# A new issue list for the same operations: fewer zero matmuls, fewer changes of tile shape on TensorE

## The chip, the core and the metric

The kernel runs on one core of one Trainium2 chip. The time is device time in microseconds (us), and a kernel's time is the median of its runs. A core has these engines, each with a queue of its own that it works through in order: TensorE (in the profile PE, its weight loads PEld), VectorE (DVE), ScalarE (ACT), GpSimd (POOL) and SyncE (SP). In this kernel SP issues every DMA. An engine waits at an instruction until the semaphores of that instruction are met, and everything behind it in the same queue waits too.

## The reference

Two unrelated layers whose outputs stand side by side in the last axis, all in float32, with 2048 positions and 576 channels each:

```
# A: a state-space convolution, N = 128 modes per channel
dt = exp(log_dt); A = -exp(log_A_real) + 1j*A_imag; C = (C_real + 1j*C_imag) * dt
K = 2*Re( sum_n C[d,n] * exp(A[d,n]*dt[d]*pos) )           # 2048 taps for each channel
y = irfft( rfft(u, 4096) * rfft(K, 4096) )[:2048] + u * D_skip

# B: linear attention, 32 heads of 18
q, k, v = x @ wqkv
phi(z) = concat( softmax(z @ w_phi), softmax(-(z @ w_phi)) )
o = phi(q) @ (phi(k)^T v)  /  ( phi(q) @ sum(phi(k)) + 1e-6 )
out = concat( y, o @ wo )
```

## The kernel before

`body` does not issue anything while it builds. It registers 2459 operations in a `Plan`, each with its engine (some with a second engine that may do it instead), what it reads and writes, and, for TensorE, the shape of the array tile that its matmuls use (`mode`, rows by columns: 128x128, 64x128, 128x32, 64x32, 32x64, 32x128, 128x64). The text `ORDER` at L992 then says in which order they are issued. `Plan.run` walks through it, and each engine gets its own operations in the order of that list. One word of `ORDER` reads like `1521@60:7`: the number is the operation, an `x` behind it gives it to its second engine, the digits behind `@` are the PSUM banks (0 to 7) for the PSUM tiles that it is the first to use, and the number behind `:` is a count of zero matmuls that `emit` puts on TensorE directly ahead of it:

```
for word in ORDER.split():
    word, _, fill = word.partition(":")
    word, _, at = word.partition("@")
    k = int(word.rstrip("x"))
    ...
    self.emit(k, o, o[12][0] if word[-1] == "x" else o[0], int(fill or 0), at)
# in emit, with fill > 0:
    for _ in range(fill):
        self.matmul(t[0:cols, 0:n], self.zero.t[0:rows, 0:cols], self.data.t[0:rows].bitcast(BF16)[:, 0:n], ...)
```

A zero matmul (L237 in the profile) multiplies a tile of zeros with the identity matrix, 256 columns, in the tile shape of the operation behind it and into that operation's own PSUM bank. It changes no result, it needs that bank to be free, and it needs none of the operation's inputs. All other matmuls stand at L295 (`mm`), transpositions at L549 and L577.

The operations, in units that the list interleaves freely:

- *fold* (four of them, at the start and in the middle): the weights of keys, values, queries and output are split in a high and a low part (`wh`, `wl` and `vh`, `vl`), the first and third multiplied with `w_phi` on the way (25 matmuls, `fT` with the staged weights).
- *key* and *query*, 16 tiles of 128 positions each. A tile loads x, splits it into `x9`, and runs two halves of 14 matmuls of 288 columns for each weight (the 28 of them are called a GEMM here; `gemm`, L410). A key tile then takes the double softmax (mostly DVE L434, L314, L437, L442, ACT L440, POOL L310 on `e`) and adds 32 small matmuls into the sums (k4, `e` with `v`). A query tile takes the softmax, transposes (q3, L549), multiplies with the sums (q4), divides, transposes (q5, L577) and runs the GEMM with `wo` (q6).
- *u* (16): the first half of the Fourier transform of u (`u_first`, 4 matmuls `ub` with `w1`, two copies, a DMA to DRAM).
- *par* and *group* (18 pairs of groups): powers and phases of the modes. Of a pair, g0 makes exponents on TensorE (`sel` with `mg`, three times two matmuls, 64x128), ACT takes their exp in PSUM (L811), POOL and ACT make sines (L757, L774 to L785), DVE multiplies them (L815, L816, L818, L820), and g4 (128x32) sums over the modes.
- *kfirst* (16) and *product* (16): the same transform of K, and for each of 16 sets of frequencies the load of its factors `ff` and of u and K (`ub`), transforms p1 and p2 (64x32), the product (DVE L314, `ac`), and p4 back (32x64). The `ff` tiles have two buffers.
- *last* (16): the result is read back from DRAM, l1 (64x32), a copy into `ot`, four DMAs of 73 KB each to the output (L979).

PSUM has 8 banks. A bank is reused when the copies out of it are done, so an operation on TensorE waits for its inputs and for the readers of the banks that the list gives it.

Of the kernel before, what the change touches and what calls it, by code (L numbers as in the profile page):

```python
# [992 lines left out]
0 1 2 3 1097 1093 4 68 1094 5 1096 1154 1104 1105 1107 1092 1108 1109 51 34 1095 6 27 7@0:49 20 1106 1110 1111 1112 1113 1114 1115 8 35@2 1199 1137 11  # L993
28@4 29 52 12 1116 1120 9 53x 30 36 10 54 13 22@6 32 37 21 1117 39 992 1118 1119 40 15@0 14 1074 23 31 33 1121 38 1063 1003 344 18 25 16 345 24
1004@42:11 19 26 17 41 1073 287 1127 1077 56@6 47 42 288 1078 48 1122 1124 346x 1123 57 347x 1125 43 1126 44 45 60 1396 1076 1084 1006 1128 1129 289x
1130 1080 61 49 1075 348@0 1400 46 1131 349 1079 290 1138 291@6 1132 1161 1133 1134 352 62 1081 292 295 353 296 1082 354 1085 351@2 1083 350 355x 1397
1048 294@0 59@6 1086 1399 1135 55 1136 63 268 269 1155 361 1005 64 58 356 69 71 270x 297 360 1162 1156 1157 1398 271x 65 1158 171 1087 1064@24 1066 72
1200 1163 293 273@6 272 357 66 67 73x 1159 1164 1160 1065 1088 298x 1089 50@4 299 358 1090 1168 74 1165 70 304 359 1166 1167 77@2 300 276 1139 1401
301 277 1402 362 172 173x 1169 1170 1192 302 76 274@0 1140 275 80 278 1141 1403 1091 1148 1147 279 1149 1150 174 303 1193 1201 1151@56 1172 111 1098
1171 81 82 1152@72 305 285x 1099 79@0 1180 1174 112 1173 1175 78 1177 1176 1153@35 89 1178@6 1067 1068 1194 1183 284 1202 1203 1181 1184 83 1204 1195  # L1000
# [94 lines left out]
```

## Time and profile before

| | |
|---|---|
| median of 3 runs | 545.37 us (543.55 to 545.37) |
| the profiled execution | 545.11 us, its span 543.3 us |
| TensorE busy | 521.5 us, 96% |
| VectorE busy | 455.9 us, 84% |
| ScalarE, GpSimd busy | 382.1 us (70%), 328.8 us (61%) |
| mean granted clock of TensorE | 0.998 |
| moved by DMA | 107.01 MB |

The span runs from the first to the last instruction of one execution. Busy time is the union of an engine's instructions; a matmul's row lasts longer than the distance to the next one (the array overlaps them), so the time that an operation costs on TensorE is read from the starts of two neighbours and not from its busy time. In a row of the order of time stand the start, the length, and in brackets the idle time ahead of the row and what ended it.

### The profile page before, as it was taken

Reading aid. Unit: us, or ns where it says so; the run is one execution under the profiler, and the core shown is the slowest. Engines: PE = TensorE matmul, PEld = TensorE weight load, DVE = VectorE, ACT = ScalarE, POOL = GpSimd, SP = SyncE. Lnnn points to the kernel's source line nnn. Section 1 sums busy time; section 2 is a strip of 40 time slices with the busy share of each in tenths; the row PEclk is TensorE's granted clock in tenths of the full one; section 3 lists DMA queues with packets and bytes.
Section 4 is the critical chain, followed back from the end, with each engine's and each line's share of the span. In section 5 each row is a group of like instructions: output and inputs, shape, how many; then the busy total and the mean of one; then the engine's idle time right before and its main releaser. Section 6 shows DMA issues by size and latency. Waiting matters only on the chain.

```text
span 543.3 us, 19242 instructions
## 1 busy us (share of the span) xinstructions
PE 521.5 (96%) x8192; PEld 435.9 (80%) x8192; DVE 455.9 (84%) x716; ACT 382.1 (70%) x555; POOL 328.8 (61%) x456
## 2 busy tenths in 40 slices
PE   8999999999999989999999999999899999999995
PEld 7999899888888767888878666766689877776984
DVE  7999899898868889999989996999974889787641
ACT  4868798798559799889689977989733444343332
POOL 1173885958777775982758998997433617434300
PEclk9999999999999999999999999999999999999999
DMA  8936711244245678246664588756458789998785
GB/s 235 326 105 195 281 45 31 101 139 134 89 139 190 207 241 294 83 128 196 229 205 118 153 265 250 241 180 194 131 173 271 234 281 293 287 281 260 265 252 157
DMA packets 86163, 107.01 MB, mean 197 GB/s; under 512 B 5698, under 2 KB 70338, under 8 KB 86078
## 3 DMA queue, kind: packets, MB, share of 16 engines
q1 hardware_dynamic: 86078, 105.79, 61.5%
q8 instruction: 64, 1.05, 0.8%
q14 instruction: 21, 0.17, 0.1%
HBM read 61.22 MB, written 44.54 MB: 195 GB/s over the span
## 4 chain that ended last, share of the span: by engine, by line
PE 69%; DVE 13%; DMA 7%; ACT 4%; issue 3%; SPq 2%; POOL 1%; DVEq 0%; ACTq 0%; POOLq 0%
PE psum L295 63%; PE psum L549 3%; DMA ff<-in_ff_dram 2%; DMA dram<-zi 2%; PE psum L237 2%; DVE ac L314 1%; DVE cs L816 1%; SPq L979 1%; PE psum L577 1%; DMA cs<-dram 1%; DVE e L310 1%; DMA ub<-dram 1%; DVE e L314 1%; DVE small L434 1%; DVE small L437 1%
## 5 line engine op out<-in xcount | busy, mean ns | idle before, releaser
L295 PE MATMUL psum<-vh,x 128*128 128x288 f32 x576 | 123.6, 301 | 0.5 <-ACT ks L300 0.5
L295 PE MATMUL psum<-wh,x 128*128 128x288 f32 x576 | 124.1, 302 | 0.0
L757 POOL TENSOR_TENSOR cs<-cs,pi 128x32 int32<-128x32 int32 (+4 forms) x180 | 108.5, 608 | 8.0
L295 PEld LDWEIGHTS psum<-wh,x 128*128 128x128 f32 x576 | 94.1, 188 | 7.7 <-issue 4.2
L295 PEld LDWEIGHTS psum<-vh,x 128*128 128x128 f32 x576 | 94.0, 188 | 5.4 <-issue 3.2
L295 PE MATMUL psum<-vl,x 128*128 128x288 f32 x320 | 93.8, 295 | 0.0
L295 PE MATMUL psum<-wl,x 128*128 128x288 f32 x320 | 93.7, 295 | 0.0
L811 ACT ACTIVATE psum<-psum 128x512 f32<-128x512 f32 x108 | 59.9, 588 | 15.4 <-PE psum L295 14.9
L295 PEld LDWEIGHTS psum<-vl,x 128*128 128x128 f32 x320 | 60.2, 188 | 0.0
L295 PEld LDWEIGHTS psum<-wl,x 128*128 128x128 f32 x320 | 60.2, 188 | 0.0
L310 POOL TENSOR_TENSOR x<-zo,x 64x128 fp32r<-64x128 f32 (+1 forms) x30 | 25.4, 848 | 46.3 <-ACT x L394 35.1
L310 POOL TENSOR_TENSOR e<-e,small 128x1152 f32<-128x1152 f32 (+1 forms) x24 | 41.2, 1720 | 14.5 <-DVE small L450 7.8
L815 DVE TENSOR_TENSOR cs<-psum,cs 128x1024 f32<-128x1024 f32 x36 | 43.6, 1212 | 3.7 <-ACT psum L811 3.6
L310 POOL TENSOR_TENSOR e<-small,e 128x576 f32<-128x576 f32 x26 | 30.6, 1177 | 25.4 <-DVE small L437 23.6
L816 DVE TENSOR_TENSOR cs<-psum,cs 128x1024 f32<-128x1024 f32 x36 | 43.6, 1214 | 1.4 <-PE psum L295 1.3
L295 PE MATMUL psum<-ub,ff 64*32 64x288 f32 x1024 | 40.0, 410 | 4.3 <-DMA ff<-in_ff_dram 1.9
L295 PEld LDWEIGHTS psum<-kvb,fT 126*128 126x128 f32 (+1 forms) x320 | 38.3, 188 | 7.2 <-issue 2.9
L295 PEld LDWEIGHTS psum<-cs 128*32 128x32 f32 x2304 | 34.1, 110 | 11.2 <-issue 2.9
L295 PE MATMUL psum<-cs 128*32 128x64 f32 x2304 | 40.0, 220 | 2.6 <-DVE cs L816 0.9
L295 PE MATMUL psum<-kvb,fT 126*128 126x133 f32 (+1 forms) x320 | 41.6, 280 | 0.1
L440 ACT ACTIVATE e<-e 128x1152 f32<-128x1152 f32 x32 | 37.0, 1164 | 2.7 <-POOL e L310 1.3
L781 ACT ACTIVATE cs<-cs 128x1040 f32<-128x1040 int32 x36 | 38.3, 1064 | 0.6 <-POOL cs L776 0.4
(156 smaller groups left out, 1115.2 us busy)
## 6 DMA issues: line engine op xcount, KB each, us to landing
dram<-zi SPq DMA_DIRECT2D x32, 576.0 KB
ub<-dram SPq DMA_DIRECT2D x64, 288.0 KB
dram<-zo SPq DMA_DIRECT2D x32, 288.0 KB
zo<-in_xT_dram SPq DMA_DIRECT2D x24, 320.0 KB
zi<-dram SPq DMA_DIRECT2D x12, 576.0 KB
ub<-in_u_dram SPq DMA_DIRECT2D x16, 288.0 KB
xd<-x SPq DMA_DIRECT2D x8, 576.0 KB
x<-xd SPq DMA_DIRECT2D x8, 576.0 KB
```

The costliest lines, as they stand in the source:

```text
L237: self.matmul(t[0:cols, 0:n], self.zero.t[0:rows, 0:cols], self.data.t[0:rows].bitcast(BF16)[:, 0:n], start=not o[13], stop=not o[13], ski ...
L295: pe.matmul(o, l, r, start=start, stop=stop, skip_group_check=skip)
L310: op(eng, [c_dve(n[0]) if e == "dve" else c_pool(n[1]) for e in eng], lambda e: (dve if e == "dve" else pool).tensor_tensor(dst(), a(), b( ...
L314: op(eng, c_dve(n) if eng == "dve" else c_pool(n), lambda: e.tensor_tensor(dst(), a(), b(), op=alu), r=r, w=w, with_=with_, lock=eng == "p ...
L434: op("dve", c_dve(D), lambda: dve.tensor_reduce(two(top.t), v(), axis=AX.X, op=ALU.max, negate=True), r=[p], w=[top])
L440: op("act", c_act(1152) + 40, lambda: act.activation(e.t, e.t, AF.Exp), r=[e], w=[e], table="exp")
L549: pe.transpose(tp.t[0:m, j - j0, :], e.t[:, sign, 7 * g:7 * g + GRP[g], :].rearrange("p h f -> p (h f)"), ident.t)
L757: op("pool", c_pool(2 * n * W), lambda n=n, j=j: pool.tensor_tensor(x()[:, :, :, n:2 * n], x()[:, :, :, 0:n], pi.t[:, j:j + 2, gs].bitcast ...
L781: act.activation(cs.t[:, 1], cs.t[:, 1].bitcast(I32), AF.Sin, scale=TURN)
L811: op("act", c_act(512), lambda b=b: act.activation(b.t, b.t, AF.Exp), r=[b], w=[b], table="exp")
L815: op("dve", c_dve(64 * W), lambda: dve.tensor_tensor(F(), both(M.t), F(), op=ALU.mult), r=[M, cs], w=[cs])
L816: op("dve", c_dve(64 * W), lambda: dve.tensor_tensor(E.t[:, :, :, 32:64], both(up.t), cs.t[:, :, :, 0:32], op=ALU.mult), r=[up, cs], w=[E])
```

## The change

Only the text `ORDER` changes, all 83 of its lines. The 2459 operations, the tiles and the buffers are the same. Counted over the two lists:

| | before | now |
|---|---|---|
| zero matmuls | 118 (49 ahead of the first fold, 69 at 12 other places, up to 11 at one) | 75 (the same 49, 26 at 17 other places, 1 to 3 at one) |
| changes of tile shape from one TensorE operation to the next | 240 | 229 |
| instructions on DVE, ACT, POOL by choice of the second engine | 716, 519, 452 | 725, 511, 451 |

The first words of the list:

```diff
-0 1 2 3 1097 1093 4 68 1094 5 1096 1154 1104 1105 1107 1092 1108 1109 51 34 1095 6 27 7@0:49 20 1106 1110 1111 1112 1113 1114 1115 8 35@2 1199 1137 11
+0 1 2 1104 4 6 1073 27 1105 1093 20 1094 1107 5 1106 68 1108 34 7@6:49 1110 51 1109 8 28@0 1111 13 1112 11 1113 9 1095 1114 12 1115 29 35@2 32 1003
...
```

Most of TensorE's operations keep their place to within a few neighbours. Three places of TensorE's queue show the kinds of move.

The start, from the end of the first fold to the first key GEMM (`w1` with `ub` is u, `wh` and `wl` with `x9` the GEMM). Before:

```order
L295 MATMUL psum_73<-fT_99,cs_177 128x126 x5
L295 MATMUL psum_73<-fT_99,e_214 128x126 x5
L237 LDWEIGHTS zero_86
L237 MATMUL psum_73<-ident_84,zero_86 128x256
...
L295 MATMUL psum_73<-ub_244,w1_225 128x288 x4
L295 MATMUL psum_73<-wh_195,x9_202 128x288
L295 MATMUL psum_73<-wl_204,x9_202 128x288
```

Now, in the same queue:

```order
L295 MATMUL psum_73<-fT_106,cs_101 128x126 x4
L295 MATMUL psum_73<-fT_106,e_179 128x126 x5
L295 MATMUL psum_73<-ub_197,w1_199 128x288 x4
L295 MATMUL psum_73<-wh_182,x9_202 128x288
L295 MATMUL psum_73<-wl_188,x9_202 128x288
```

The 11 zero matmuls between fold and u are gone (the rows left out of the first list repeat its pair). On DVE, one operation of 1536 elements (`sel`, L310) that stood behind the first fold's `fT` is now done by POOL.

The middle, around the exponents of the pair of groups 8 (`sel` with `mg` is g0, `cs` with `cs` is g4, `ub` with `w1` is u, `wh` and `wl` with `x9` the query GEMMs). Before:

```order
L295 MATMUL psum_73<-ub_3031,w1_225 128x288 x4
L295 MATMUL psum_73<-sel_109,mg_1819 128x512 x4
L237 LDWEIGHTS zero_86
L237 MATMUL psum_73<-ident_84,zero_86 128x256
...
L295 MATMUL psum_73<-ub_3170,w1_225 128x288 x4
L237 LDWEIGHTS zero_86
L237 MATMUL psum_73<-ident_84,zero_86 128x256
...
L295 MATMUL psum_73<-sel_109,mg_1819 128x512 x2
L295 MATMUL psum_73<-cs_3326,cs_2976 32x64 x32
L295 MATMUL psum_73<-wh_2835,x9_3304 128x288
```

Now:

```order
L295 MATMUL psum_73<-sel_210,mg_1824 128x512 x2
L295 MATMUL psum_73<-ub_2862,w1_199 128x288 x4
L237 LDWEIGHTS zero_86
L237 MATMUL psum_73<-ident_84,zero_86 128x256
L295 MATMUL psum_73<-sel_210,mg_1824 128x512 x2
L295 MATMUL psum_73<-ub_2810,w1_199 128x288 x4
L295 MATMUL psum_73<-wh_2931,x9_3233 128x288
...
L295 MATMUL psum_73<-wl_2984,x9_3233 128x288
L295 MATMUL psum_73<-sel_210,mg_1824 128x512 x2
L295 MATMUL psum_73<-cs_3304,cs_2808 32x64 x32
```

The 8 and 7 zero matmuls there become 1 (and 2 ahead of the first `sel`), and half a GEMM (14 matmuls) of query tile 3 now stands between the second u and the last `sel`, ahead of g4.

Later, the transposition of query tile 6 (L549) between the exponents of the pair of groups 17. Before:

```order
L295 MATMUL psum_73<-ac_5307,ff_5146 64x288 x16
L295 MATMUL psum_73<-sel_109,mg_4641 128x512 x2
L549 MATMUL psum_73<-ident_84,e_4532 126x128 x4
L295 MATMUL psum_73<-sel_109,mg_4641 128x512 x2
L549 MATMUL psum_73<-ident_84,e_4532 126x128 x4
L549 MATMUL psum_73<-ident_84,e_4532 72x128 x2
```

Now:

```order
L295 MATMUL psum_73<-ac_5257,ff_5040 64x288 x16
L295 MATMUL psum_73<-sel_210,mg_4690 128x512 x4
L549 MATMUL psum_73<-ident_84,e_4501 126x128 x4
L549 MATMUL psum_73<-ident_84,e_4501 72x128 x2
L549 MATMUL psum_73<-ident_84,e_4501 126x128 x4
```

The two pairs of `sel` now stand together ahead of the three transpositions, which makes two changes of tile shape fewer there.

More of the change, by code (lines that the diff above doesn't have):

```diff
@@ L997 @@
[L997 to L1000, printed above, removed]
@@ L1073 @@
[L1073 to L1075 removed]
+0 1 2 1104 4 6 1073 27 1105 1093 20 1094 1107 5 1106 68 1108 34 7@6:49 1110 51 1109 8 28@0 1111 13 1112 11 1113 9 1095 1114 12 1115 29 35@2 32 1003
+992 30 52 1120 22@4 36 1116 1096 10 1092x 344 53 37 21 44 3 39 14@6 15 1161 47 31 23 25 33 38 40 1004@02 1097 1117 16 1154 24 26 1006 54 1076 345 1118
@@ new lines @@
+308 1049@62 1254@5 1418 1050 100 1283x 1229@67 101 1307 1051 1420 1098 225 1282 340x 226x 198@2 1421 1257 102 1258 1008 1306 1260 196@0 1261 199 103x
+1255x 197 229 1284 208 1262 1263@5 209 1265@67 1422 200 1440 1052 201 1069@20 343 1285 1314 1308 249 1264 202 1071 1313 1267@51 1439 195 1309 1070
+1423 1288 1266@06 1315 1286 104 1424 1296 203 1310 1311 309x 1316 1287 1317 1289 105 1294 98@2 1318 99 204 1312 1290 1291 250 1319 1067 109 1297
+1292@7 1300 1425 1320 1293x 1299 1426 106 1427 1103 230 310@2 1039@60 311 1484 205 1321 206 1428 108 379x 1295 1041x 1322 207x 314 107 231 313@0 232
@@ new lines @@
+402 458 389@4 1468 1010 1445@23 1527 1472 404 1528 406 1474 1535 1469 1475 405 1473 408 1012 407 1470@6 1361 1537 388 1536x 1471x 390 1478 395@0 392
+1362 1363 396 410@6 409 1476 399 1364 1365 397 1037 1477 1366 1479@2 400 1369 393 391 371@3 411 415 1368 367@4 398 374x 413 1370 459@0 414 1371 373x
+993 1367 1429 1538 412 460 368x 1372 365 1480x 1430 1373 1374 1431 372x 1376 424 1375x 461 426@6 462 370 526 416 994@02 369x 425 1432 375 417
+1519@54:2 463 1433 996x 995x 427 1044@20 1377 464 428 377 1539 1520@76:1 1045x 376 997 1434 429 1046 1548 430 1542 1541 1540 1551 1435 378 1545
@@ new lines @@
+2155 1741 1751 2046 2111 2157 1742 2162@0 1612@45 567 1724 1632 2161 604 557 558 1743 662 2163 568 517@23 1725 1633 605 2047 1635 630@0 518 1753 519
+2048 520 1744 1752x 1636 1613@46 1614@72 521 1634 1641 1637 2164 1638 629 1639@3 569 523@4 1643 1642 1644 522 2165 631 2053 1784 1646 632 2051@0 1783
+1754 1647 1640x 1735@63 457 1645 1785 1786 1648@2 606 633 1755 1787 607@7 1788 1789 524 1791x 1649 2052x 1756 570 2166@04 608 1758 1776 571 1736@72
+611@6 2167 2049@4 1777 1759 2168 1757 1761 1778 1779 1780 1781 2109 1760 609@3 1764 2050 2116 1773@01 610 1737@45 1782 1794 2110 612x 1765 1766
@@ L1076 @@
+2425@4 954 2406 2407 989@2 2426x 2428 2408 2427 2430 988 990 2429 991
 """
```

146 lines of the change are left out of this document (68 added, 78 removed).

## The prediction

> **What bounds the kernel now.** I read the page's busy times and its chain first, then the busy time by stretches, then TensorE's rows in order of time at the places that the list changes.
>
> ```profile
> PE 521.5 (96%) x8192; PEld 435.9 (80%) x8192; DVE 455.9 (84%) x716; ACT 382.1 (70%) x555; POOL 328.8 (61%) x456
> PEclk9999999999999999999999999999999999999999
> PE 69%; DVE 13%; DMA 7%; ACT 4%; issue 3%; SPq 2%; POOL 1%; DVEq 0%; ACTq 0%; POOLq 0%
> ```
>
> TensorE is busy 96% of the span and makes 69% of the chain. DVE's 13% of the chain says that TensorE often stands behind DVE. By stretches (columns: length, then busy us and instructions of PE, PEld, DVE, ACT, POOL; clock, DMA share, GB/s):
>
> ```profile
> 8.90:100.00 91.10, 90.40 (x1281) 84.77 (x1282) 86.44 (x131) 72.80 (x99) 53.32 (x86) 1.00 0.49 162
> 200.00:250.00 50.00, 47.89 (x626) 41.44 (x616) 47.06 (x92) 44.98 (x62) 37.59 (x53) 1.00 0.59 191
> 250.00:300.00 50.00, 48.60 (x761) 40.71 (x766) 47.41 (x83) 42.75 (x63) 30.97 (x52) 1.00 0.54 170
> 300.00:350.00 50.00, 48.78 (x927) 34.19 (x912) 44.46 (x63) 41.99 (x65) 45.84 (x60) 1.00 0.79 239
> 350.00:400.00 50.00, 47.05 (x983) 33.67 (x985) 48.11 (x69) 42.41 (x64) 36.35 (x47) 1.00 0.48 151
> ```
>
> Up to 100 us TensorE has almost no idle time (0.7 of 91.1 us). From 200 to 400 us DVE is busy 47.06 + 47.41 + 44.46 + 48.11 = 187.0 of 200 us, so there TensorE and DVE bind together: a us taken from TensorE alone can turn into a wait for DVE. 52 of the 69 later zero matmuls lie in this stretch.
>
> **The zero matmuls.** All of them in one group, then two of the 12 places where they stand:
>
> ```profile
> L237 PE MATMUL psum<-ident,zero 128*128 128x256 bf16 (+5 forms) x118 | 17.0, 294 | 2.0 <-DVE zero L333 1.6 <-DVE zi L300 0.2 <-DVE zo L604 0.2
> ...
> 14.60 1.26 PE L237 MATMUL psum<-ident,zero 64*128 64x256 bf16 x10
> 15.60 0.51 PE L295 MATMUL psum<-ub,w 64*128 64x288 f32 x1
> ...
> 16.87 0.40 PE L295 MATMUL psum<-wh,x 128*128 128x288 f32 x1
> ...
> 305.00 1.37 PE L237 MATMUL psum<-ident,zero 64*32 64x256 bf16 x11
> 306.23 1.15 PE L295 MATMUL psum<-ub,ff 64*32 64x288 f32 x25
> ```
>
> Ten of them take 1.26 us, the last one's length (0.27 us, the group's 294 ns at most) included, so one costs (1.26 - 0.27) / 9 = 0.11 us of TensorE. The list has 69 - 26 = 43 fewer: 4.7 us if each stood on the path, nothing if each stood in a wait that stays. At 14.60 and 305.00 (11 each) the operation behind starts at once and no row shows that it would have waited; 7 more, ahead of product 8 at 382 us, are like that. That is 29 of 69, or 3.2 us. The other 40 stand where the next row below them waits anyway. If the 26 of the new list divide in the same way, 11 cost 1.2 us. I take -2.0 us for this term, between -4.7 and 0.
>
> At the start the gain must not be lost at once. After u come the first key GEMM's halves, which need `wl` from DVE:
>
> ```profile
> 14.41 2.02 DVE L367 TENSOR_TENSOR wl<-psum,wh 128x288 fp32r<-128x288 f32 x5
> ```
>
> DVE ends the last low part at 16.43 us, and the GEMM starts at 16.87. Its first half needs only the first three of five blocks of weights, so it may start near 15.8, when u ends without the zero matmuls, and run 1.9 us before the second half needs the last block. DVE also loses `sel` (1.75 us) ahead of these rows. So 1.1 of the 2.0 us lies here and I count it as nearly safe; the rest lies in the stretch of 200 to 400 us.
>
> **The changes of tile shape.** The 32 small matmuls of a key tile (k4), once before another shape and once before the same shape:
>
> ```profile
> 79.78 0.75 PE L295 MATMUL psum<-e,v 128*19 128x36 f32 x64
> 80.46 0.40 PE L295 MATMUL psum<-vh,x 128*128 128x288 f32 x1
> ...
> 93.48 0.72 PE L295 MATMUL psum<-e,v 128*19 128x36 f32 x62
> 94.02 0.23 PE L295 MATMUL psum<-cs 128*32 128x64 f32 x1
> ```
>
> From start to start k4 takes 0.68 us before a 128x128 matmul and 0.54 before g4, which has its shape: 0.14 us a change, nothing beside it on TensorE. 11 fewer changes are 1.5 us; taking 0.1 to 0.14 us each (a change after other operations may cost less), -1.1 to -1.5, I take -1.3. Nine of the 11 fall away before 200 us by TensorE's own work, where little else binds.
>
> **The waits that move.** Most of the neighbourhoods are the same, so I compare the places of the largest waits. Around the pair of groups 8:
>
> ```profile
> 213.12 0.50 PE L295 MATMUL psum<-sel,mg 64*128 64x512 f32 x2 [0.80 <-DVE e L314]
> 213.79 1.03 PE L237 MATMUL psum<-ident,zero 64*128 64x256 bf16 x8 [0.16 <-DVE zi L300]
> 214.66 1.19 PE L295 MATMUL psum<-ub,w 64*128 64x288 f32 x7
> ...
> 216.31 0.96 PE L295 MATMUL psum<-sel,mg 64*128 64x512 f32 x2
> 218.16 0.54 PE L295 MATMUL psum<-cs 128*32 128x64 f32 x24 [0.89 <-DVE cs L816]
> ...
> L300 ACT ACTIVATE zi<-psum 128x576 f32<-128x576 f32 x41 | 25.8, 649 | 18.5 <-PE psum L295 13.3 <-DVE e L310 3.9 <-DMA dram<-zi 0.8
> ```
>
> g4 starts 1.85 us after the last `sel`, which alone takes 0.4: a wait of 1.4 us for DVE's last product. In the new list half a query GEMM (1.9 us) stands in that gap, so the 1.4 us go. But this GEMM takes bank 0, which the u just ahead of it has filled, and so waits for u's copy: estimate 0.9 us, from ACT's 0.65 us a copy and the matmuls' tail of 0.3. Net -0.5. The queue behind it, the last `sel` and g4, waits with it.
>
> At the transposition of query tile 6:
>
> ```profile
> 356.00 0.50 PE L295 MATMUL psum<-sel,mg 64*128 64x512 f32 x2
> 357.54 0.66 PE L549 MATMUL psum<-ident,e 128*126 128x128 f32 x4 [1.04 <-DVE ac L314]
> ...
> 356.13 1.36 DVE L314 TENSOR_TENSOR ac<-ac,psum 128x1152 f32<-128x1152 f32 x1 [0.19 <-PE psum L295]
> 357.40 1.22 DVE L815 TENSOR_TENSOR cs<-psum,cs 128x1024 f32<-128x1024 f32 x1
> ```
>
> It waits 1.04 us for a bank that DVE reads until 357.5. In the new list it has another bank, but its second part (two matmuls of 72 rows) takes a bank of the first `sel` just ahead, which DVE's L815 frees at 358.6 in these rows. The wait changes its name and not its length: 0 to -0.3.
>
> The loads of the factors stay as they are. In the chain:
>
> ```profile
> 437.14 4.07 DMA ff<-in_ff_dram
> ...
> 474.50 4.36 DMA ff<-in_ff_dram
> ```
>
> An `ff` load is issued when the product two before it has ended on TensorE, and lands 4.1 to 4.4 us later. Counting TensorE's operations between that end and the new product's p1 by their starts in this trace, products 8, 11, 12 and 14 have 2.6, 2.7, 3.4 and 4.1 us before, and 2.3, 3.4, 2.9 and 4.1 us now. The sum is the same to 0.1 us, so these waits stay, 0.
>
> Counting all PSUM banks in this way, 44 of 505 reuses follow the last matmul of the bank's former use by under 1 us before, 46 now; under 2 us it is 181 and 195. So the list is no looser. For the net of the waits I take -0.7 us. Before, by the distance of starts over that of the same operation in its fastest tenth, TensorE loses over 0.25 us at some 30 places, 23 us in all, 0.75 each; if as many fall at other places, the sum differs by about the root of 30 times 0.75, 4 us either way.
>
> **The other engines.** DVE gets nine instructions more and ACT eight fewer. Of the key tiles' last multiplication DVE does 8 instead of 4:
>
> ```profile
> L310 POOL TENSOR_TENSOR e<-e,small 128x1152 f32<-128x1152 f32 x12 | 27.3, 2272 | 7.9 <-DVE small L450 7.8
> L310 DVE TENSOR_TENSOR e<-e,small 128x1152 f32<-128x1152 f32 x4 | 5.7, 1426 | 0.1
> L310 DVE TENSOR_TENSOR sel<-cst 128x1536 fp32r<-128x1536 f32 x1 | 1.8, 1752 | 0.0
> L310 DVE TENSOR_TENSOR x<-zo,x 128x512 fp32r<-128x512 f32 x13 | 10.0, 772 | 0.2 <-ACT x L394 0.2
> L300 DVE COPY v<-psum 128x576 f32<-128x576 f32 x4 | 3.0, 755 | 2.1 <-PE psum L295 1.1 <-ACT zi L300 1.0
> ```
>
> That is +5.7 us, less `sel` (1.75), and less six subtractions of 0.77 us of key tiles that go to POOL and three copies of 0.75: about -2 us for DVE in the key tiles. The later tiles and products give it about +6.5 us of rows (softmax and product terms, copies). It has 13 us free from 200 to 400 us, so I cost this at nothing; without that cover it is the slower rival below.
>
> **The end.**
>
> ```profile
> 525.55 12.56 SPq L979 DMA_DIRECT2D out_dram<-ot  x18
> ```
>
> SP issues the last outputs one behind the other, 0.7 us each. Behind its last load from DRAM stand 22 issues before and 21 now: 0, at most -0.7.
>
> **The sum.** -2.0 - 1.3 - 0.7 = -4.0 us against the profiled execution's 545.11 (span 543.3 and 1.8 around it): 541.1, and since the median is 0.26 us above it, 541.4 us.
>
> [...] The longest idle time of TensorE between matmuls:
>
> ```profile
> 281.84 0.48 PE L295 MATMUL psum<-ub,ff 64*32 64x288 f32 x8 [1.18 <-DMA ub<-dram]
> ```
>
> It is 1.18 us, with no zero matmul ahead of it, and the clock's line is full in all 40 slices, also where waits stand without zero matmuls. So with 43 fewer of them I expect the clock to stay, and cost it at 0. [...]
>
> **The rivals.**
>
> (a) The forecast, 541.4, 538.5 to 543.5 by itself. Chance 0.47.
>
> (b) The zero matmuls stood in waits that remain, and DVE keeps TensorE waiting from 200 to 400 us. For it speaks DVE's 94% there. Only the start (-1.1) and some changes of shape (-0.5) are left: 543.8 us. Chance 0.26.
>
> (c) The waits fall too, as the fewer and shorter fills would have it if each count stood for a gap that the list really has: -4.7 - 1.3 and -2 of waits, 537.4 us. Against it speak the equal counts of tight banks. Chance 0.11.
>
> (d) Slower: DVE becomes the bound from 200 to 400 us. Its 6.5 us more then come onto the path as far as they exceed the slack, and decide once its share there passes some 97% (6 of the 13 free us used up by order, not by load). With all of them, and -1.1 and -0.9 left from the first 200 us: 549.9; with half of them, 546.6 us. Chance 0.14.
>
> [...] Chance 0.02.
>
> **How the numbers follow.** No change and a change of 0.5% (2.7 us) can hardly be told apart here, so 542.6 and 548.1 are the bounds. Faster: most of (a), 0.42, and (c), 0.11, together 0.53. The same: the rest of (a), 0.05, (b), (e) and a little of (d), 0.02, together 0.35. Slower: the rest of (d), 0.12. The range, 537 to 546.5, reaches from just below (c) to (d) with half its price and takes in the 4 us of the waits; it leaves out a sixth.
>
> **What would show it.** L237 has 75 instructions. The first key GEMM starts near 15.8 us instead of 16.87. From 8.9 to 100 us TensorE does about 2 us more of the list than before. g4 of the pair 8 follows the last `sel` without a wait, with one ahead of the query GEMM instead. The `ff` waits are still there, the clock is full, and DVE's share from 200 to 400 us is at most 95%. I am wrong if DVE is at 97% there and TensorE's idle time has grown, if the first GEMM waits for POOL's `sel` or subtraction, or if new waits for banks of over 1 us stand at more than a few places.

## The result, and the profile after

The changed kernel takes 569.58 us (median of 4 runs, 566.22 to 572.55) against 545.37 us before on the same chip: 1.0448 times as long, 95% interval 1.0383 to 1.0513. It is slower by 24 us where 4 us less were forecast. The profiled execution has a span of 568.6 us, 25.3 us more than before.

The page after, answering to the first lines shown of before:

```profile
PE 531.6 (93%) x8149; PEld 440.5 (77%) x8149; DVE 484.7 (85%) x725; ACT 377.9 (66%) x547; POOL 336.0 (59%) x455
PEclk9999899999999999897999999999899999999989
```

Two things stand out. DVE is busy 28.8 us longer (455.9 to 484.7) with nine instructions more. And the clock's line is no longer full: slices 4, 16, 18, 28 and 38 of the 40 (counted from 0) show an 8 or a 7.

The same stretches as before (length, then busy us and instructions of PE, PEld, DVE, ACT, POOL; clock, DMA share, GB/s):

```profile
8.90:100.00 91.10, 84.59 (x1144) 79.41 (x1142) 87.74 (x128) 67.94 (x90) 59.16 (x87) 0.98 0.53 172
200.00:250.00 50.00, 46.11 (x646) 38.69 (x647) 45.28 (x75) 42.97 (x67) 37.30 (x53) 0.93 0.56 187
250.00:300.00 50.00, 47.37 (x578) 39.79 (x584) 46.59 (x80) 37.27 (x55) 29.52 (x44) 0.93 0.55 182
300.00:350.00 50.00, 47.67 (x884) 33.37 (x883) 46.96 (x69) 44.19 (x66) 44.83 (x59) 1.00 0.54 167
350.00:400.00 50.00, 47.65 (x913) 34.41 (x912) 46.14 (x65) 44.69 (x61) 41.82 (x60) 1.00 0.65 206
```

Up to 100 us TensorE now idles 6.5 of 91.1 us (0.7 before) and gets through 1144 matmuls where it did 1281, zero matmuls included. DVE does 128 instructions in 87.74 us there, 0.69 us each; before it did 131 in 86.44, 0.66 each. A busy share hides this: it stays in the nineties (94.9 and 96.3%) while each instruction takes longer.

Where the 25.3 us lie on TensorE: its idle time (span less busy) goes from 21.8 to 37.0 us, +15.2. It runs at half clock for 27.3 us ahead of the end, which makes its own work up to 13.7 us longer. The zero matmuls take 10.0 instead of 14.5 us, -4.5. That is +24.4 us. Adding up every operation of TensorE at the fastest length of its kind in the traces gives 469.0 us before and 468.0 now; this is the 11 changes of tile shape, -1.0 us. So TensorE's own work became a little shorter, as forecast, and its waiting and its slow running come to up to 29 us. Summed over the rows of its waits, those for DVE (without the wait for the tile of zeros at the start) grow from 5.4 to 16.9 us, those for ACT and POOL from 4.0 to 6.1; those for DMA fall from 3.8 to 2.9. The largest (the view of TensorE's waits: us in total, times, longest):

```profile
PE psum L295 <- DVE e L310: 3.5, 2, 2.2
PE psum L295 <- DVE zi L300: 3.3, 3, 1.8
PE psum L295 <- issue: 2.1, 2, 1.8
PE psum L295 <- DMA zi<-dram: 1.8, 1, 1.8
```

The loss builds up from the start. At equal work done on TensorE (its operations weighted by their fastest lengths in both traces) the changed kernel is behind by 1.2 us when before stands at 51 us, 9.2 at 115, 12.9 at 158, 13.4 at 231, 20.5 at 275, 22.1 at 416 and 26.1 at 531. Half of it is there by 158 us, ahead of the stretch in which I had looked for the danger.

**What became longer on DVE.** Four groups of instructions of before, by line and form (times, busy us, mean ns, idle time ahead):

```profile
L314 DVE TENSOR_TENSOR ac<-ac,psum 128x1152 f32<-128x1152 f32 x24 | 31.7, 1348 | 8.2 <-ACT ac L300 5.7 <-PE psum L295 2.3
L732 DVE TENSOR_SCALAR ot<-pi 128x384 f32<-128x384 f32 x6 | 2.1, 352 | 0.1
L314 DVE TENSOR_TENSOR mn<-ax,ay 128x192 f32<-128x192 f32 x3 | 1.1, 353 | 0.5 <-ACT ay L690 0.5
L521 DVE TENSOR_SCALAR e<-e 18x35 f32<-18x35 f32 x1 | 0.2, 190 | 0.0
```

and the same groups after:

```profile
L314 DVE TENSOR_TENSOR ac<-ac,psum 128x1152 f32<-128x1152 f32 x24 | 32.0, 1347 | 3.9 <-PE psum L295 3.3 <-ACT ac L300 0.2
L732 DVE TENSOR_SCALAR ot<-pi 128x384 f32<-128x384 f32 x6 | 4.3, 722 | 0.1
L314 DVE TENSOR_TENSOR mn<-ax,ay 128x192 f32<-128x192 f32 x3 | 3.1, 1038 | 0.0
L521 DVE TENSOR_SCALAR e<-e 18x35 f32<-18x35 f32 x1 | 2.3, 2286 | 0.0
```

`ac`, which reads PSUM, keeps its length to the nanosecond. The three that read and write SBUF alone take two to twelve times as long, with the same shapes and counts. Over all of DVE's groups, those with a PSUM input hold 451 instructions and 334.7 us before, 455 and 334.8 after. Those without hold 265 and 159.2 us before, 270 and 191.0 after: the whole growth, 31.8 us, is theirs.

Why they are longer is in the order of time (start, length; in brackets the idle time ahead and what ended it), after:

```profile
219.16 2.29 POOL L383 TENSOR_TENSOR vl<-e,vh 128x960 fp32r<-128x960 f32 x1 [0.28 <-ACT vh L382]
219.21 2.29 DVE L521 TENSOR_SCALAR e<-e 18x35 f32<-18x35 f32 x1
...
222.35 1.40 DVE L300 COPY zi<-psum 128x576 f32<-128x576 f32 x2
223.14 0.51 PE L295 MATMUL psum<-ub,w 64*128 64x288 f32 x1 [1.21 <-DVE zi L300]
...
258.40 2.26 POOL L383 TENSOR_TENSOR vl<-e,vh 128x960 fp32r<-128x960 f32 x1
258.58 2.29 DVE L314 TENSOR_TENSOR pa<-ay,ax 128x192 f32<-128x192 f32 x1
...
260.80 0.74 DVE L300 COPY zi<-psum 128x576 f32<-128x576 f32 x1
261.60 0.52 PE L295 MATMUL psum<-ks,kf 32*128 32x288 f32 x3 [1.82 <-DVE zi L300]
```

Both DVE instructions start just behind one of POOL's and end 0.05 and 0.21 us after it (POOL's end at 221.45 and 260.66 us), whatever their own size: 18 by 35 elements take 2.29 us, and 128 by 192 take 2.29 as well. One is a `TENSOR_SCALAR` (L521, 0.19 us before, at 206.3 us, where POOL is idle from 204.98 to 207.25), the other a `TENSOR_TENSOR` with both inputs in SBUF (`pa`, L314, 0.48 us in the mean of three before). DVE's reductions and reciprocals, which have one input, keep their length beside POOL: at 118.60 us a reduction (L437) takes 0.74 us though POOL works on `e` up to 120.73 (all 32 of its kind take 0.69 to 0.76), and at 54.50 a reciprocal (L450) takes 0.54 us beside POOL's L757 of 54.33 to 55.14 (all 16 take 0.54 to 0.55). The copies `zi` stand behind the long instruction on DVE (the second starts at 260.80, as `pa` ends at 260.87), so they free their banks some 2 us late (an estimate: 2.29 less 0.19 or 0.48), and TensorE waits 1.21 and 1.82 us.

I call such a lengthening beside POOL a clash below. In the list before it was almost avoided. Measured against the shortest instruction of the same line, operands and shape in the same kernel, 6 of DVE's instructions are over 0.4 us too long before and 27 after, 3.4 and 24.9 us in all, and none of them has a PSUM input. One of the six of before, with POOL's row ahead of it:

```profile
207.25 2.29 POOL L383 TENSOR_TENSOR vl<-e,vh 128x960 fp32r<-128x960 f32 x1 [2.27 <-ACT vh L382]
...
208.70 1.25 DVE L314 TENSOR_TENSOR pi<-pi,ot 128x384 f32<-128x384 f32 x1
```

The price could have been read there. The kernel itself marks these operations at L315 (`lock=eng == "pool" or not any(x.tag == "ps" for x in r)`), so whoever wrote the list before could have kept them apart; whether that was done is not shown.

**What fell to half clock.** Two of the places (length, busy of PE, PEld, DVE, ACT, POOL, clock):

```profile
54.21:57.62 3.41, 1.10 (x99) 0.92 (x99) 3.41 (x6) 3.39 (x5) 2.82 (x5) 1.00 0.92 247
57.62:61.03 3.41, 3.41 (x64) 2.66 (x50) 3.38 (x6) 2.62 (x5) 2.67 (x5) 0.50 0.68 271
221.46:224.87 3.41, 2.20 (x12) 1.12 (x11) 3.32 (x7) 3.38 (x4) 1.56 (x2) 1.00 0.14 49
224.87:231.70 6.83, 6.02 (x24) 4.77 (x23) 6.73 (x9) 5.01 (x8) 4.42 (x6) 0.50 0.98 334
```

The first row of each pair is the 3.41 us ahead of the fall, the second the fall itself. TensorE was busy 32% and 64% of the time just before. The first has the wait of 2.16 us behind another clash (DVE's `mn`, 1.74 us at 52.84 beside POOL's `e` of 52.17), the second the 1.21 us above.

### The profile page after: what moved, and what is told of

Same layout as the page of the kernel before. It is cut to its first block, busy times and chain, and to the rows that moved or that the text cites. A ratio compares the mean times of both kernels' runs of the same rounds, so it can differ in the third digit from the quotient of the medians.

```text
span 568.6 us, 19154 instructions
## 1 busy us (share of the span) xinstructions
PE 531.6 (93%) x8149; PEld 440.5 (77%) x8149; DVE 484.7 (85%) x725; ACT 377.9 (66%) x547; POOL 336.0 (59%) x455
## 5 line engine op out<-in xcount | busy, mean ns | idle before, releaser
L295 PE MATMUL psum<-vh,x 128*128 128x288 f32 x576 | 125.7, 304 | 0.1
L757 POOL TENSOR_TENSOR cs<-cs,pi 128x64 int32<-128x64 int32 (+4 forms) x180 | 111.2, 628 | 6.2
L295 PEld LDWEIGHTS psum<-wh,x 128*128 128x128 f32 x576 | 94.9, 190 | 8.5 <-ACT zi L300 2.0
L295 PEld LDWEIGHTS psum<-vh,x 128*128 128x128 f32 x576 | 95.8, 191 | 6.5 <-issue 2.7
L445 POOL TENSOR_TENSOR o<-e 128x576 f32<-128x576 f32 x16 | 21.9, 1366 | 45.4 <-ACT e L440 45.3
L295 PEld LDWEIGHTS psum<-kvb,fT 126*128 126x128 f32 (+1 forms) x320 | 40.6, 197 | 7.1 <-issue 3.9
L310 POOL TENSOR_TENSOR x<-zo,x 128x512 fp32r<-128x512 f32 (+1 forms) x31 | 29.5, 951 | 27.8 <-ACT x L394 25.1
L300 ACT ACTIVATE zi<-psum 128x576 f32<-128x576 f32 x40 | 25.1, 649 | 28.7 <-PE psum L295 25.7
L295 PE MATMUL psum<-kvb,fT 126*128 126x133 f32 (+1 forms) x320 | 43.9, 288 | 0.0
L310 POOL TENSOR_TENSOR e<-small,e 128x576 f32<-128x576 f32 x25 | 30.5, 1222 | 22.6 <-DVE small L437 19.5
L295 PE MATMUL psum<-cs 128*32 128x64 f32 x2304 | 41.5, 223 | 1.8 <-DVE ks L300 0.8
L310 POOL TENSOR_TENSOR e<-e,small 128x576 f32<-128x576 f32 (+1 forms) x20 | 31.7, 1586 | 14.5 <-DVE small L314 8.8
```

Of the source, the lines that this page charges most:

```text
L295: pe.matmul(o, l, r, start=start, stop=stop, skip_group_check=skip)
L300: op(("act", "dve"), (c_act(n), c_dve(n)), lambda e: act.activation(dst(), src(), AF.Copy) if e == "act" else dve.tensor_copy(dst(), src() ...
L310: op(eng, [c_dve(n[0]) if e == "dve" else c_pool(n[1]) for e in eng], lambda e: (dve if e == "dve" else pool).tensor_tensor(dst(), a(), b( ...
L445: op("pool", c_pool(470), lambda: pool.tensor_tensor(pair.t, e.t[:, :, :, 0:9], e.t[:, :, :, 9:18], op=ALU.add), r=[e], w=[pair], lock=True)
L757: op("pool", c_pool(2 * n * W), lambda n=n, j=j: pool.tensor_tensor(x()[:, :, :, n:2 * n], x()[:, :, :, 0:n], pi.t[:, j:j + 2, gs].bitcast ...
```

## The experiments

All in one table: median, ratio to the kernel before in the same comparison with its 95% interval (before stood at 544.6 to 545.9 us in all of them), and from the profile DVE's busy time and TensorE's waits for DVE (without the tile of zeros).

| | us | ratio | DVE busy | waits for DVE |
|---|---|---|---|---|
| before | 545.37 | | 455.9 | 5.4 |
| after | 569.58 | 1.0448 (1.0383 to 1.0513) | 484.7 | 16.9 |
| e1 before, fewer zeros | 551.52 | 1.0111 (1.0090 to 1.0131) | 457.3 | 8.2 |
| e2 after, 12 moved | 561.54 | 1.0275 (1.0233 to 1.0318) | 477.2 | 15.0 |
| e3 after, zeros in waits | 567.09 | 1.0388 (1.0345 to 1.0430) | 484.1 | 17.2 |
| e4 before, then new | 562.63 | 1.0311 (1.0286 to 1.0337) | 472.3 | 9.3 |
| e5 after, zeros of before | 575.99 | 1.0549 (1.0497 to 1.0601) | 486.8 | 20.3 |
| e6 after, engines of before | 598.72 | 1.0982 (1.0946 to 1.1018) | 473.0 | 32.7 |
| e7 TensorE's list alone | 699.81 | 1.2820 (1.2754 to 1.2885) | 461.3 | 60.6 |
| e8 after, 21 moved | 563.56 | 1.0321 (1.0254 to 1.0389) | 473.1 | 11.6 |
| e9 before, clashes put in | 553.24 | 1.0150 (1.0119 to 1.0181) | 461.3 | 11.2 |
| e10 after, 64 moved | 566.38 | 1.0376 (1.0338 to 1.0414) | 478.8 | 17.9 |
| e11 before, 50 moved | 553.24 | 1.0149 (1.0105 to 1.0193) | 459.1 | 9.6 |
| e12 after, 86 of DVE moved | 563.79 | 1.0354 (1.0309 to 1.0400) | 481.2 | 19.3 |
| e13 before, 115 moved | 555.12 | 1.0186 (1.0148 to 1.0223) | 466.6 | 12.0 |
| e14 after, 141 moved | 569.69 | 1.0449 (1.0416 to 1.0481) | 482.6 | 23.0 |
| e15 before, POOL's reads away | 543.55 | 0.9965 (0.9942 to 0.9988) | 449.5 | 4.9 |
| e16 after, POOL's reads away | 547.06 | 1.0044 (1.0012 to 1.0075) | 452.8 | 3.8 |
| e17 e9, POOL's reads away | 543.79 | 0.9983 (0.9959 to 1.0007) | 449.6 | 4.6 |

### The zero matmuls by themselves

**e1: the list of before without its 69 later zero matmuls.**

```diff
-1004@42:11   -1014@24:8   -1521@60:7
+1004@42      +1014@24     +1521@60
... (12 words, 69 zero matmuls)
```

> The list of before with the 69 later zero matmuls left out and nothing else changed. Theory A (the new list is slow because instructions of DVE stand against instructions of POOL, which makes DVE late and TensorE wait, and the waits then make the clock fall): the zero matmuls matter little, 541 to 547 us, with at most two pieces of half clock of 3.4 us before the end. Rival B (the zero matmuls held the clock up, and 43 fewer of them are the cause): four or more pieces of half clock, 552 us or more.

Measured: 551.52 us, 1.0111, between the two ranges, with 6.8 us at half clock ahead of the end. Taking away work on TensorE made the kernel 6.1 us slower. Where the eleven stood ahead of u (14.60 in the rows of before), e1 has:

```profile
13.83 1.17 PE L295 MATMUL psum<-fT,e 126*128 126x126 f32 x9
15.91 0.51 PE L295 MATMUL psum<-ub,w 64*128 64x288 f32 x2 [0.91 <-DVE wl L367]
```

u starts at 15.91; with the zero matmuls it started at 15.60. They had covered a wait of the same length, and a wait that is covered by fill has no row. At product 2 (p2, 310.2 us) the operation ahead is 1.36 us longer where 1.25 us of zero matmuls went. These two places hold 22 of the 69, and I had priced them in full. From the start of the operation ahead to the start of the one behind, e1 saves 0.13 us at the first and loses 0.14 at the second. At four places with 28 zero matmuls (8 at 213.79 us, 7 ahead of product 8 at 382, 7 at 384 and 6 at 440) it saves 0.50 to 0.87 us each, 2.5 us together; three of these I had priced at nothing. So most of the 69 hid a wait, and the rows of before did not tell which. In all, TensorE's idle time grows from 21.8 to 31.5 us, more than the 7.2 us of zero matmuls that went. What then made it slower is less clear: TensorE's waits for DVE grow by 2.8 us and those for ACT, POOL and DMA stand at 6.5 and 5.7 us (4.0 and 3.8 before), at other places, and 6.8 us run at half clock, in the slice from 220 to 234 us (a 7 in the clock's line).

**e5: the changed list with the zero matmuls of before in place of its own.**

```diff
-1004@02      -1014@02     -1521@56     -1444@67:1
+1004@02:11   +1014@02:8   +1521@56:7   +1444@67
... (the 12 words of before, the 17 of the new list without)
```

> The new list with its own 26 later zero matmuls taken out and the 69 of before put in, each count ahead of the same operation as in the list of before. Theory A (instructions of DVE that stand behind POOL's make the loss): these stand at places where the new list does not wait, so little changes, 566 to 572 us. Rival B (fewer zero matmuls are the loss): 560 to 564, since leaving the 69 out of before cost 6 us.

Measured: 575.99 us, 1.0549 (1.0497 to 1.0601), above both ranges and some 6 us over the changed kernel; the two intervals just meet. So in the new list the same zero matmuls seem to cost time; that the waits which they covered now lie elsewhere is the likely reason and not shown. That the new list is slow for want of them is not borne out.

**e3: the changed list with 53 zero matmuls in three of the new waits** (k4 at 57.3 us, g0 at 125.5, the end at 548.5).

```diff
-305      -1265@67      -2432@0
+305:20   +1265@67:17   +2432@0:16
```

> The new list with zero matmuls put into three of its long waits, whose banks are free by then: 20 ahead of the small matmuls of key tile 12 (57 us), 17 ahead of the first exponents of pair 3 (125 us), 16 ahead of the last transform 12 (548 us). The waits themselves stay. If half clock costs half of its 3.4 us each (theory A's second step): these three pieces go, 5.1 us less, 562.5 to 566.5. If the clock falls only while TensorE waits anyway, and costs nothing: 568 to 572.

Measured: 567.09 us, 1.0388 (1.0345 to 1.0430), between the two ranges. In the profiled executions the time at half clock falls from 27.3 to 6.8 us, the median only by 2.5 us, which the intervals do not tell from nothing. That is less than the 10 us that half of the difference would be, but the 53 zero matmuls are work too, and other runs speak for a higher price. In the four runs of the changed kernel the time follows the mean granted clock: 566.22 us at 0.982, 572.55 at 0.973, which is some 10 us more at half clock (one less the clock, times twice the span) for 6 us more time. In e4 it is 561.06 us at 0.987 and 563.22 at 0.972, some 17 us for 2 us. What half clock costs by itself stays open; that the falls stand behind waits is read from the windows ahead of them, above (waits of 2.16 and 1.21 us, TensorE busy 32% and 64%).

### Where in the list the time goes

**e4: the first 700 words of before, then the rest in the order of the changed list.**

> The first 700 words of the list of before (to about 160 us), and then what is left in the order of the new list. If each loss is local (theory A, and C): the 12 us lost by the new list up to there go, with the pieces of half clock near 57 and 126 us; 556 to 560 us. If an early lateness of one engine carries on through the whole list: 564 or more, since what comes behind is unchanged; and if the first part only shifts the losses: 569.

Measured: 562.63 us, between the ranges. The first 160 us run as before (within half a us), the rest loses some 18 us, where the new list loses 13 behind its own first 160 us. The loss belongs to no one place, and the second part does not lose the same behind another first part.

**e6: the changed list with before's choice of engine for all 135 operations that differ; e7: only TensorE's operations in the new order, the others near their places of before.**

```diff
-1092x  -53   -346   -347   (e6, four of 135)
+1092   +53x  +346x  +347x
```

> The new list in its order, with all 135 operations whose engine the two lists choose differently done by the engine of before. Theory A (the order on DVE and POOL makes the clashes): most of the loss stays, 562 to 572 us. Rival D (the load does it: nine more instructions on DVE and other shares for POOL): 548 to 556.

> TensorE's part of the new list alone: its order of operations, banks and zero matmuls, while DVE, ACT, POOL and the DMA queue keep the engines and the order of before as far as what TensorE needs allows (31 of 716 operations on DVE, 13 on ACT, 9 on POOL and 2 DMAs stand out of that order). Theory A (the loss is in DVE's and POOL's order): 546 to 555 us, and DVE's instructions are hardly longer than before. Rival C (TensorE's order and banks): 562 or more.

Measured: 598.72 and 699.81 us. Both were meant to split the change into TensorE's order and the others', and both missed. e6 lies far outside both ranges; e7 lies where rival C (TensorE's order and banks) was forecast, but 130 us above the changed kernel, so it does not tell what made that one slow. An operation given to another engine, or an engine left in the old order, stands in queues that do not fit, and TensorE waits 32.7 and 60.6 us for DVE. They show only that the parts of the list depend on each other, and leave TensorE's order neither blamed nor cleared. DVE's busy time falls to 473.0 and 461.3 us in them and the time rises, so that busy time alone does not decide.

### Clashes taken out by moving words

**e2: the changed list with 12 of DVE's operations moved by a few words, away from the POOL operation that each met; e8: nine more, and a load of `mg` issued earlier, which I took g0 at 125.53 to wait for.**

```diff
-277 1401 301 ... 76 1402 278 ... 302 1048
+277 301 ... 76 278 ... 302 1401 1402 1048
... (e2: also 375, 1410, 1418, 1420, 1421, 1432, 1433, 1690, 1694 to 1696; 13 words in the whole list)
```

> The new list with 12 DVE instructions moved behind later ones of DVE, so that they no longer stand beside POOL's long instructions just ahead of what TensorE waits for (parameters of blocks 2, 3 and 4, and the small addition of kv). No TensorE operation, bank, zero matmul or choice of engine changes. Theory A: the waits near 57, 116, 223 and 261 us shrink by 1 to 2 us each, 6 to 8 us in all, and three of the six pieces of half clock go (1.7 + 3.4 + 3.4 us): 553 to 560 us. Rival B: 567 to 571, the pieces of half clock stay. Rival C (the banks and the order on TensorE make the waits): 565 or more.

> The kernel with 12 DVE instructions moved, and a second round of the same: 9 more DVE instructions of parameters moved behind others that read PSUM (near 14, 18, 22, 118 and 250 to 260 us), and one load of the exponents' table (mg, block 1) issued next to that of its other half. Theory A: 4 to 8 us less than with the first round, 553 to 558 us. Rivals: the first round's gain was a chance, 560 or more.

Measured: e2 561.54 us, 1.0275 (1.0233 to 1.0318), 8 us of the 24 back; e8 563.56, 1.0321 (1.0254 to 1.0389), not to be told from e2. DVE is busy 7.5 us less in e2 and 11.6 less in e8. e2 gains a little less than forecast, and e8's median is what I had set down for a chance gain. By the count of above, 24 clashes are left in e2 and 18 in e8, of 27: more than half of those taken away at one place turned up at another, since every shift moves what runs beside what. And e8, with the fewest, is not the faster one: number of clashes and time do not go together one for one, presumably since a clash costs time only where TensorE comes to wait for what stands behind it.

**e10: 64 of DVE's operations moved in the changed list, and the same load of `mg`; e12: 86 of DVE's alone, their places picked from the lengths and waits in three traces; e14: from e8's list and picked in the same way, 141 operations of all engines (nine of TensorE) and eight choices of engine.**

```diff
-30 52 1120 22@4 ... 1097 1117 16 1154 24 26 1006
+30 1120 52 22@4 ... 1097 16 1154 1137 24 26 1117 1006
... (e10, two of 64 moves)
```

> The new list with TensorE's part, every engine's choice, and ACT's and POOL's order as they are; 64 DVE instructions stand at other places of DVE's order (40 of them parameters), so that by the trace's times none starts while POOL works on SBUF, and the load of mg's block 1 stands earlier, as in the second round. Theory A: DVE's instructions are about as long as in before, and most of the 24 us go: 543 to 553 us. Rival C: what two rounds of moves left, 558 or more.

> The new list with DVE's order alone changed, now with places picked from the durations and waits in the traces of three runs (the new list, the first and the second round of moves): 86 of 725 DVE instructions stand elsewhere in DVE's order, everything else word for word. Theory A (clashes of DVE with POOL, and DVE working on things that can wait while TensorE waits for it): DVE's busy time comes down from 484.7 to 465 us or less, TensorE's waits for DVE from 17 to under 10 us, and the kernel takes 548 to 557 us. Rival C (TensorE's order, banks and zero matmuls): 560 or more although DVE's busy time is down.

> The kernel of the second round of moves (the new list), with places picked in the same way on all engines: against the new list 61 DVE, 17 ACT, 30 POOL, 24 DMA and 9 TensorE operations stand elsewhere in their engine's order, 8 are done by the other engine; 472 of TensorE's 481 operations, the banks and the zero matmuls are those of the new list. Theory A: 540 to 550 us. Rival C: 556 or more.

Measured: 566.38, 563.79 and 569.69 us, all above what theory A forecast and where rival C lay (in e12 on condition that DVE's busy time came down). But DVE is still busy 478.8, 481.2 and 482.6 us, with 25, 22 and 30 clashes: none of them took the clashes away. They are misses as tests of the theory, since what they set out to remove is still there; the time stayed with it.

**e11: the list of before with 29 operations of DVE, 13 of ACT and 8 of POOL moved by the rule of e10; e13: 115 operations of all engines (11 of TensorE) and 13 choices of engine, picked as in e12.**

```diff
-1104 1105 1107 ... 27 7@0:49 ... 1106 1110
+1104 1107 ... 27 1105 7@0:49 ... 1106 52 1110
... (e11, two of 50 moves)
```

> The list of before with 29 DVE, 13 ACT and 8 POOL instructions at other places of their engine's order, by the same rule (no DVE instruction without PSUM starts beside POOL's), TensorE's list word for word. Theory A: before has few clashes, so little is left to win, 540 to 545 us. It is also the control for moving as such: if moving that many instructions by a few places costs of itself, 548 or more.

> The list of before with places picked in the same way, on all engines: 43 DVE, 21 ACT, 22 POOL, 18 DMA and 11 TensorE operations stand elsewhere in their engine's order, 13 are done by the other engine. If the order on DVE and POOL is what these kernels lose time by: 537 to 543 us, faster than before. If moving costs of itself, as the tidied list of before made it look (553): 548 or more.

Measured: 553.24 and 555.12 us, both slower than before, as forecast if moving operations cost of itself. They do not settle that, since they brought clashes in: 11 and 12 where before has 6. But they warn that 8 us more can come of moving some fifty operations, and so e9 below needs a counterpart. No re-ordering that I tried, of either list, came to the time of before.

### Clashes put in, and POOL's reads taken away

**e9: the list of before with 12 of DVE's operations on modes (*par*) moved behind starts of POOL operations.**

```diff
-290 1138 291@6 ... 1048 294@0 ... 1157 1398 271x ... 1066 72
+290 291@6 ... 1048 1138 294@0 ... 1157 271x ... 1066 1398 72
... (also 1139, 1401, 1402, 1403, 1419, 1432, 1690, 1693, 1694, 1721)
```

> The list of before with 12 DVE instructions moved (additions and roundings of the parameters of blocks 1, 2, 4 and 5, none needed soon by TensorE) to places just behind the start of a POOL instruction; nothing else, TensorE's list word for word. Theory A: each of them, 0.34 to 0.55 us long before, lasts until POOL's instruction ends; DVE's instructions get some 6 to 8 us longer in all, what stands behind them on DVE comes late, and the kernel takes 550 to 556 us. Rival C (the loss is in TensorE's order, banks and zero matmuls): 544 to 547, as before.

Measured: 553.24 us, 1.0150 (1.0119 to 1.0181): 8 us for twelve moves that touch neither TensorE's order nor a choice of engine nor a zero matmul. One of the moved operations beside POOL's, in e9:

```profile
98.67 2.19 POOL L310 TENSOR_TENSOR e<-e,small 128x1152 f32<-128x1152 f32 x1
...
98.81 2.47 DVE L314 TENSOR_TENSOR pi<-pa,steps 128x384 f32<-128x384 f32 x1
```

By line, the six of these in e9:

```profile
L314 DVE TENSOR_TENSOR pi<-pa,steps 128x384 f32<-128x384 f32 x6 | 6.2, 1040 | 0.0
```

and the same six in e17 (below), the same list without POOL's reads:

```profile
L336 DVE TENSOR_TENSOR pi<-pa,steps 128x384 f32<-128x384 f32 x6 | 3.2, 540 | 0.0
```

The median is in the range forecast. Moving DVE's operations could also cost by their later results. The next three runs tell this apart.

**e15, e16, e17: before, after and e9, each with POOL's reading of SBUF taken away.** They leave out part of the computation: POOL's sums, products and copies are not done. In their place POOL fills the output with a constant, or works on one element of each row where it works in place. All instructions, their order, their engines and what they wait for stay (line numbers are 22 higher).

```diff
+class Short:
+    def tensor_tensor(self, out, a, b, op):
+        if ...:                                   # out is also an input
+            self.e.tensor_tensor(self.cut(out), self.cut(a), self.cut(b), op=op)
+        else:
+            self.e.memset(out.bitcast(F32), 1.0)
+    def tensor_copy(self, out, a):
+        self.e.memset(out.bitcast(F32), 1.0)
...
-    pe, dve, act, pool, sp = nc.tensor, nc.vector, nc.scalar, nc.gpsimd, nc.sync
+    pe, dve, act, pool, sp = nc.tensor, nc.vector, nc.scalar, Short(nc.gpsimd), nc.sync
```

> The list of before, with POOL's two-input instructions and copies replaced: where POOL works in place it does one element of a row, elsewhere it fills its result with a constant, so that POOL reads almost nothing from SBUF (its sums, products and copies are left out of the computation). Every order, bank, engine and wait is as before. It is the base for the next two. Theory A and rival C: 530 to 545 us, DVE's busy time a little under 455.9.

> The new list with POOL's instructions replaced in the same way (same parts of the computation left out). Theory A (the clashes of DVE with POOL's reading make most of the loss): DVE's busy time falls by 20 us or more, and the distance to the list of before with the same replacement is 0 to 10 us instead of 24. Rival C (TensorE's order, banks and zero matmuls, or DVE's order by itself): the distance stays 16 us or more.

> The list of before with the 12 DVE instructions moved (553 us with POOL as it is), and POOL's instructions replaced in the same way. If the clashes made its 8 us: within 2 us of the list of before with the same replacement. If moving instructions costs of itself: 6 us or more above it.

Measured: 543.55, 547.06 and 543.79 us, each in the range forecast for the clashes. The busy times of e15:

```profile
PE 521.2 (96%) x8192; PEld 434.8 (80%) x8192; DVE 449.5 (83%) x716; ACT 380.9 (70%) x555; POOL 108.1 (20%) x456
```

of e16:

```profile
PE 519.9 (95%) x8149; PEld 433.9 (79%) x8149; DVE 452.8 (83%) x725; ACT 375.9 (69%) x547; POOL 113.7 (21%) x455
```

and of e17:

```profile
PE 523.2 (96%) x8192; PEld 436.8 (81%) x8192; DVE 449.6 (83%) x716; ACT 381.3 (70%) x555; POOL 108.1 (20%) x456
```

The kernel before gains 1.8 us of median by it, the changed kernel 22.5, e9 9.5. The distance of after to before shrinks from 24.2 to 3.5 us, that of e9 from 8 to 0.2. The groups without a PSUM input sum to 152.0 us in e15 and 159.0 in e16 (159.2 and 191.0 with POOL's reads), so clashes lengthen DVE by 7.2 us before and 31.9 after, and the instructions that the new list adds to DVE are worth 7.1 us. In e16 the groups shown above are back at their lengths:

```profile
L754 DVE TENSOR_SCALAR ot<-pi 128x384 f32<-128x384 f32 x6 | 3.5, 588 | 0.1
L336 DVE TENSOR_TENSOR mn<-ax,ay 128x192 f32<-128x192 f32 x3 | 1.1, 350 | 0.0
L543 DVE TENSOR_SCALAR e<-e 18x35 f32<-18x35 f32 x1 | 0.2, 181 | 0.0
```

All but one of the six `ot`: it takes 1.56 us at 264.92 (0.35 at 277.68), beside a row of POOL's fills from 264.87 to 267.24, so this `TENSOR_SCALAR` is longer beside POOL's writes as well. With POOL's reads these runs also take away two thirds of POOL's busy time, 328.8 to 108.1 us, and with it any wait for a long POOL instruction. e15 bounds that for the list of before: all of it together is worth under 2 us there. For the new list the two are not told apart as cleanly. But its waits for POOL were small: TensorE's for POOL and ACT together are 6.1 us after and in e16, and DVE's for POOL 3.6 us after, less than the 7.8 of before. TensorE's waits for DVE fall from 16.9 to 3.8 us in e16, below the 4.9 of e15. Some 20 of the 24 us thus go with POOL's reads. Within these bounds, most of them are the clashes and what follows from them, the half clock included (27.3 us of it after, 10.2 in e16).

What stays: 3.5 us by which e16 is slower than e15, 1.0044 against 0.9965. The new list on TensorE, without clashes, is not faster either.

## Why the prediction was wrong

**The step that failed** is that of the other engines: "It has 13 us free from 200 to 400 us, so I cost this at nothing". It counted the instructions that change engine (about -2 and +6.5 us, where the terms written there add up to -2.9 and not -2; e16 against e15 gives +7.1 for the groups without PSUM) and priced each at its mean of before. But a DVE instruction of these kinds on SBUF has no length of its own: it has one alone and another behind a POOL instruction (0.19 and 2.29 us at L521), and which it gets is decided by the order of the two queues against each other. The term left out was +24.7 us of DVE (31.9 less 7.2), some +20 of time. I judged the list by TensorE's neighbourhoods, where 150 of 481 operations are out of order between the two lists. On DVE it is 266 of the 657 that it does in both, and I did not look at what stands beside POOL's long instructions. The 1.25 us at 208.70, where the same operation takes 0.55 in the mean without POOL's reads (e16), stood in before's rows.

**The zero matmuls**, -2.0 forecast, between -4.7 and 0. All 69 gone cost 6.1 us (e1), outside the ends. That no row shows a wait was read as that there was none; but fill hides the row, and of the places priced in full the two largest gave nothing, while three priced at nothing gave 2 us. At the start, the 1.1 us that I had called nearly safe were worth 0.15: the first key GEMM starts at 16.72 (before 16.87, forecast 15.8), since already its first half waits for `wl`.

```profile
16.72 0.40 PE L295 MATMUL psum<-wh,x 128*128 128x288 f32 x1 [0.26 <-DVE wl L367]
```

**The changes of tile shape**, -1.3 forecast: -1.0 by the sums of fastest lengths. Right, and drowned.

**The waits that move**, -0.7 with 4 us either way: the sum of TensorE's idle time grew by 15.2. At the named places it went as said. At the pair 8 the half GEMM waits for ACT's copy in bank 0 (0.9 forecast) instead of g4 for DVE; at query 6 the 1.04 us wait got another name and 0.86 us:

```profile
228.84 0.61 PE L295 MATMUL psum<-wh,x 128*128 128x288 f32 x1 [0.57 <-ACT zi L300]
...
377.14 0.49 PE L295 MATMUL psum<-sel,mg 64*128 64x512 f32 x2 [0.86 <-DVE ac L314]
```

In these places the wait could be forecast from neighbours. The large ones arose elsewhere: of the eight waits of over 1 us behind the start (three before), four are for a late DVE at `e` and `zi`, and a fifth for DVE's `vl`.

**The loads `ff`**, 0: not so, in the small. TensorE's waits for them fall from 1.9 us (three) to none in the view, most likely because TensorE comes later to those products. And g0 at 125.53 waits 1.83 us for which the trace names no releaser (`issue`). I had put it down to its load of `mg`, issued at 114.81 us where before issued it at 106.9; but that load's last landing in the trace is at 120.60, and with it issued earlier (e8) g0 still waits 1.14 us there. This cause is open.

**The clock**, 0, from a longest wait of 1.18 us and a full line before: wrong. It fell six times, with no gap over 2.16 us. In this trace all six falls start on one grid, at 57.62 us and 20, 49, 60, 102 and 144 times 3.4133 us later, and last 3.413 or 6.827 us. TensorE was not idle ahead of them: in the 3.41 us before each it was busy 32 to 64% of the time.

**The rivals.** (d) comes nearest by its sign, with DVE as the cause, but not by its mechanism: it asked for DVE's share to pass 97% from 200 to 400 us. The share is 92.5% (45.28 + 46.59 + 46.96 + 46.14 of 200), below before's 93.5, and half the loss lies ahead of 200 us. (e), at 0.02, is the rival with a falling clock, and no run shows the term that it was priced by: the clock fell six times, in windows whose longest waits were 0.86 to 2.16 us, for 27.3 us in all. (b)'s doubt of the zero matmuls was right for most of them. Of the signs that I had named, the 75 zero matmuls (L237) came and TensorE's idle time grew, but DVE's share did not reach 97%; and of the new waits of over 1 us only the two behind `zi` are for banks. Up to 100 us the list does not gain 2 us on before but falls 7 us behind.

## What to carry to other kernels

Before an order of issue is changed, list for DVE which two-input instructions and which `TENSOR_SCALAR` use SBUF alone, and for POOL which read SBUF and for how long (2.19 to 2.29 us in the rows shown here), and lay the two queues side by side: the length of the first kind depended on the order here (0.19 or 2.29 us for the same 18 by 35 elements), and a busy share did not show it, only the mean of each group did. Zero matmuls hid the wait behind them (69 of them gone made e1 6.1 us slower), so their removal could not be priced from the trace that contains them; take them out of the old list first and run that. And this list, tuned as a whole, had no separable parts: seven re-orderings meant to better one list or the other (e2, e8, e10 to e14) were all slower than before.

## What the runs showed of the hardware

A DVE instruction of 18 by 35 elements took 0.19 us alone and 2.29 us when it started 0.05 us behind a POOL instruction of 2.29 us; with a PSUM input, `ac` kept its length in both lists (1348 and 1347 ns over 24), and so did reductions and reciprocals on SBUF beside POOL (0.74 us at 118.60, where the shortest of its kind takes 0.69; 0.54 us at 54.50, where the shortest takes 0.54).

TensorE fell to half clock (matmuls 0.24 us apart at 229.25 to 230.93 instead of 0.13 at 231.81) without a gap over 2.16 us. The windows of 3.41 us ahead of the six falls had it busy 32, 40, 47, 49, 54 and 64%, with the longest gap between 0.86 and 2.16 us. The share alone does not decide it: this window, busy 52%, was followed by full clock:

```profile
497.94:501.35 3.41, 1.77 (x21) 1.33 (x27) 3.14 (x8) 2.12 (x4) 1.03 (x1) 1.00 0.99 316
501.35:504.76 3.41, 3.41 (x112) 1.91 (x100) 2.03 (x3) 1.19 (x2) 0.37 (x1) 1.00 0.93 332
```

while the one with 64% was followed by a fall. What decides it stays open.
